# A decode-attention kernel whose tensor-engine work becomes one loop of seven rounds

## The chip, the core and the metric

One core of a Trainium2 chip runs the whole kernel. The metric is the time of one execution on the device in microseconds (us), the median of several. The span in a profile is about 2 us shorter than that time (252.3 against 254.14 us in the profiled run of the kernel before). A core has five engines, each with its own instruction stream: PE (matrix multiply), DVE (vector), ACT (scalar functions), POOL (general), SP (here it only issues transfers). Sixteen transfer (DMA) engines move data between the device memory (HBM) and the core's SBUF. PE writes to PSUM; the kernel uses eight banks of 128 x 2 KB there.

## The reference

Two independent attention layers, A and B, each decoding one token. Both have 32 query heads, 16 key/value heads of 128 columns, a cache of 8192 positions, a 576-wide input. A looks only at the last 2048 positions, B at all of them.

```python
q = x @ wq                                  # 576 -> 32 heads x 128
k, v = cache (A: the last 2048 rows; B: all 8192), each head shared by 2 query heads
p = softmax(q @ k.T * 128 ** -0.5)
out = (p @ v).reshape(1, 4096) @ wo         # 4096 -> 576
result = concatenate([A, B])
```

All tensors are bf16. About 102.8 MB have to be read: 20 blocks of K and 20 of V of 2 MB each (4 of each for A, 16 for B), and four weight matrices of 4.7 MB.

## The kernel before

A small scheduler (`Program`) holds a list of operations with the resources they read and write, and derives the semaphore waits. Each engine has one semaphore that only counts up, so a wait is "at least n", once per dependency:

```python
def run(name, eng):
    seen = {}
    for op in per[name]:
        want = {}
        for o in op.deps:
            key = ("d", o.dma_sem) if o.dma_sem is not None else ("e", o.eng)
            want[key] = max(want.get(key, 0), o.value)
        for key in sorted(want):
            if seen.get(key, 0) >= want[key]:
                continue
            ...
            eng.wait_ge(sem, want[key])
        ins = op.fn(eng)
        ...
```

All loads go through a ring of 6 SBUF slots of 2 MB. For K, PE turns each block round (64 transposes of 128 x 128 through four PSUM banks, which ACT and DVE copy out to `kt`) and multiplies it with the queries. For V, PE multiplies with the transposed probabilities. Everything is written out in order, nothing is looped:

```python
def k_phase(P, c, between):
    pend = None
    for i in range(NS[P]):
        s = load_kv(ks, P, c, i)
        for half in range(2):
            u = k_transpose(s, half)          # 32 transposes, 4 copies
            if pend is not None:
                k_scores(P, *pend)
            pend = (i, half, u)
        between(i)                            # V blocks of the chunk before
    k_scores(P, *pend)
    return softmax_exp(P, c)

q_phase(0)
pa = k_phase(0, 0, lambda i: None)            # A: 4 K blocks
q_phase(1)
pb0 = k_phase(1, 0, between_b0)               # B, first 4096 rows; 3 of A's V blocks between
...                                           # cut: B's second chunk, output weights of A,
                                              # the last 8 V blocks, output weights of B
```

Of the kernel before, what the change touches and what calls it, by code (L numbers as in the profile page):

```python
# [6 lines left out]
U32 = mybir.dt.uint32  # L7
# [12 lines left out]
NSLOT = 6  # L20
NKT = 3
TS = 64
WQ_UNITS = 9
WQ_SLOT = 4
OUTW = DM // 4


class Op:
    def __init__(self, eng, fn, reads, writes, dma_sem=None):
        self.eng, self.fn, self.reads, self.writes = eng, fn, reads, writes  # L30
        self.dma_sem = dma_sem
        self.deps = []
        self.needed = False
        self.value = None


class Program:

# [4 lines left out]
    def __init__(self, nc):  # L43
        self.nc = nc
        self.ops = []
        self.writer = {}
        self.readers = {}
        self.sems = {e: nc.alloc_semaphore("done_" + e) for e in self.ENGINES}
        self.dma_sems = {}
        self.dma_count = {}  # L50

    def add(self, eng, fn, reads=(), writes=(), dma=None, after=()):
        op = Op(eng, fn, tuple(reads), tuple(writes), dma)
# [19 lines left out]
        for o, raw in deps:  # L73
            if o is op:
                continue
            if o.dma_sem is None and o.eng == eng and (not raw or eng in ("pe", "sp")):
                continue
            op.deps.append(o)
            o.needed = True
        if dma is not None:  # L80
            if dma not in self.dma_sems:
                self.dma_sems[dma] = self.nc.alloc_semaphore("dma_" + dma)
                self.dma_count[dma] = 0
            self.dma_count[dma] += 16
            op.value = self.dma_count[dma]
        self.ops.append(op)
        return op

    def emit(self):
        count = {e: 0 for e in self.ENGINES}  # L90
        for op in self.ops:
            if op.dma_sem is None and op.needed:
                count[op.eng] += 1
                op.value = count[op.eng]
        per = {e: [o for o in self.ops if o.eng == e] for e in self.ENGINES}

        def run(name, eng):
            seen = {}
            for op in per[name]:
                want = {}  # L100
                for o in op.deps:
                    key = ("d", o.dma_sem) if o.dma_sem is not None else ("e", o.eng)
                    want[key] = max(want.get(key, 0), o.value)
                for key in sorted(want):
                    if seen.get(key, 0) >= want[key]:
                        continue
                    seen[key] = want[key]
                    sem = self.dma_sems[key[1]] if key[0] == "d" else self.sems[key[1]]
                    eng.wait_ge(sem, want[key])
                ins = op.fn(eng)  # L110
                if op.dma_sem is not None:
                    ins.then_inc(self.dma_sems[op.dma_sem], 16)
                elif op.needed:
                    ins.then_inc(self.sems[op.eng], 1)
# [23 lines left out]
def bass_concat_heads__sliding_block_cached__gqa_block_cached__decode_kernel(  # L138
# [19 lines left out]
    S_len = [W_A, SK]  # L158
    base = [SK - W_A, 0]
# [3 lines left out]
    PH = [128 // G[P] for P in range(2)]  # L163
    CH = [TS * PH[P] for P in range(2)]
    NCH = [S_len[P] // CH[P] for P in range(2)]
    UW = [8 * PH[P] for P in range(2)]
    CW = [2 * UW[P] for P in range(2)]
    NS = [HKV // G[P] for P in range(2)]
# [4 lines left out]
    slots = nc.alloc_sbuf_tensor("slots", [128, NSLOT, SLOT], BF16)  # L173
    kt = nc.alloc_sbuf_tensor("kt", [128, NKT, UNIT], BF16)
    ptm = nc.alloc_sbuf_tensor("ptm", [128, 2, 32 * 512], BF16)
# [7 lines left out]
    qtm = nc.alloc_sbuf_tensor("qtm", [128, 2, HKV * 32], BF16)  # L183
    xtwo = nc.alloc_sbuf_tensor("xtwo", [128, 2, 8], BF16)
    xpad = nc.alloc_sbuf_tensor("xpad", [128, 2, 10, 32], BF16)
    par = [None, None, nc.alloc_sbuf_tensor("par2", [128, 2], F32), None, nc.alloc_sbuf_tensor("par4", [128, 4], F32)]
# [3 lines left out]
    acc = nc.alloc_sbuf_tensor("acc", [128, 3, DH], F32)  # L190
# [9 lines left out]
    misc_bf = misc[:, :].bitcast(BF16)  # L200
# [17 lines left out]
    def setup(pool):  # L218
        def zero(t):
            return pool.memset(t, 0.0)  # L220
        zero(ident[:])
        zero(xpad[:])
        zero(selq[:])
        pool.memset(onesf[:], 1.0)
        zero(warm[:])
        return zero(qtm[:])

    add("pool", setup, writes=["ident", ("xpad", 0), ("xpad", 1), "selq", "ones", "warm", ("qtm", 0), ("qtm", 1)])
# [7 lines left out]
    for b in range(2):  # L236
        for h in range(8):
            add("pool", lambda pool, b=b, h=h: pool.memset(ptm[:, b, h * 2048:(h + 1) * 2048].bitcast(U32), 0),  # L238
                writes=[("ptm", b)])

    def setup2(pool):
        pool.memset(identf[:], 0.0)
        pool.memset(pick[:], 0.0)
        pool.memset(same[:], 0.0)
        return pool.memset(opj[:], 0.0)

    add("pool", setup2, writes=["identf", "pick", "same", ("opj", 0), ("opj", 1)])
# [3 lines left out]
    for dj in range(-3, 4):  # L251
        add("pool", select(same[:], 32 * dj, [[-1, 128]], 1), reads=["same"], writes=["same"])

    for n in (2, 4):
        add("dve", lambda dve, n=n: dve.tensor_reduce(par[n][:, :], ident[:, :].rearrange("p (m g) -> p g m", g=n),
                                                      AX.X, ALU.add),
            reads=["ident"], writes=[("par", n)])

    add("act", lambda act: act.activation(warm[:, 4:8], warm[:, 0:4], ACT.Exp), reads=["warm"], writes=["warm2"])


    slot_n = [0]

    def load(src_of, view_of, what):
        s = slot_n[0] % NSLOT
        slot_n[0] += 1
        res = ("slot", s)
        add("sp", lambda sp: sp.dma_start(view_of(slots[:, s, :]), src_of()), writes=[res], dma="slot%d" % s)
        return s

    def load_wq(P, k):
        lo, hi = k * WQ_SLOT * 2048, min(WQ_UNITS, (k + 1) * WQ_SLOT) * 2048
        return load(lambda: wqs[P].rearrange("(m r) n -> m (r n)", m=64)
                    .rearrange("m (e y) -> (m e) y", e=2)[:, lo:hi],
                    lambda v: v[:, 0:hi - lo], "wq")

    def load_kv(arrs, P, c, i):
        r0 = base[P] + c * CH[P]

        def src():  # L280
            a = arrs[P]
            return a[0, i * G[P]:(i + 1) * G[P], r0:r0 + CH[P], :].rearrange("g (p t) d -> p g (t d)", t=TS)
        return load(src, lambda v: v, "kv")


    def load_wo(P, lo, parts):
        s = slot_n[0] % NSLOT
        slot_n[0] += 1
        o, made = 0, []
        for k, rows in enumerate(parts):  # L290
            n = rows * DM
            res = ("slot", s) if len(parts) == 1 else ("slot", s, k)

            def go(sp, lo=lo, n=n, o=o):
                return sp.dma_start(slots[:, s, o:o + n],
                                    wos[P].rearrange("(p j) n -> p (j n)", p=128)[:, lo * DM:lo * DM + n])
            add("sp", go, writes=[res], after=[("slot", s)], dma="slot%d" % s if res == ("slot", s) else "part%d_%d" % (s, k))
            made.append((lo, lo + rows, s, o, res))
            lo += rows
            o += n  # L300
        return made


    def x_columns(P):
        for e in range(2):
            add("dve", lambda dve, e=e: dve.tensor_scalar(xpad[:, P, 5 * e:5 * e + 5, 0], xtwo[:, P, 0:5],  # L306
                                                          par[2][:, e:e + 1], None, ALU.mult),
                reads=[("xtwo", P), ("par", 2)], writes=[("xpad", P)])
# [4 lines left out]
    def q_part(P, k, s):  # L313
        def mm(pe):
            for u in range(k * WQ_SLOT, min(WQ_UNITS, (k + 1) * WQ_SLOT)):
                for c in range(2):
                    for j in range(4):
                        n = 2 * j + c
                        x = u // 2 if n // 4 == u % 2 else 5 + (u + 1) // 2
                        o = (u - k * WQ_SLOT) * 2048 + (n % 4) * 512  # L320
                        ins = pe.matmul(qps[c][32 * j:32 * j + 32, :], lhsT=xpad[:, P, x, :],  # L321
                                        rhs=slots[:, s, o:o + 512], start=(u == 0), stop=(u == WQ_UNITS - 1))
            return ins
        add("pe", mm, reads=[("xpad", P), ("slot", s)], writes=qbank)

    def q_finish(P):
# [11 lines left out]

        def put(dve):
            row = 2 * HKV * 32  # L340
            for e in range(2):
                dst = bass.AP(tensor=qtm, offset=P * HKV * 32 + e, ap=[[row, 128], [34, 4], [136, 4]])
                src = opsum[:, 0:32].rearrange("p (a e j) -> p a e j", a=4, e=2)[:, :, e, :]
                ins = dve.tensor_copy(dst, src)
            return ins
        add("dve", put, reads=[B_O], writes=[("qtm", P)])


    k_count = [0]

    def k_transpose(s, half):
# [181 lines left out]
    def k_phase(P, c, between):  # L533
        pend = None
        for i in range(NS[P]):
            s = load_kv(ks, P, c, i)
            for half in range(2):
                u = k_transpose(s, half)
                if pend is not None:
                    k_scores(P, *pend)  # L540
# [92 lines left out]
```

## Time and profile before

| | before |
|---|---|
| time, median of 3 (lowest to highest) | 254.39 us (254.33 to 254.62) |
| span of the profiled run | 252.3 us |
| read from HBM | 102.76 MB |
| busy share: PE, DVE, ACT | 66%, 32%, 35% |
| instruction fetches of PE's queue | 27 packets, 0.44 MB |
| last output weights: first engine done, last engine done | 242.9 us, 249.2 us |
| span's end after the last landing | 3.1 us |

Lines of the profile's page. Each digit is the busy share of one of 40 slices of the span (6.3 us each), in tenths; PEclk is the granted PE clock in tenths; GB/s is what the DMA engines moved in each slice. The last two lines are DMA queues with packets, MB and their share of the sixteen engines' span.

```profile
PEclk9999999999979999599998897789997755555557
DMA  7999999999999999999999999999999999999971
GB/s 273 400 450 418 431 431 407 433 431 423 420 434 423 421 434 418 423 434 420 423 431 426 418 431 429 423 418 439 423 422 423 428 423 429 426 426 425 415 309 56
...
q1 hardware_dynamic: 7936, 102.77, 96.4%
q8 instruction: 27, 0.44, 0.7%
```

The transfers run without a gap at about 425 GB/s. The reader should look at the last two numbers, 309 and 56: the transfers fade out instead of stopping.

The same place in windows of 1 us, the last three columns being the granted clock, the busy share of the DMA engines, and GB/s:

```profile
242.00:243.00 1.00, 0.84 (x4) 0.70 (x4) 0.12 (x1) 0.00 (x0) 0.00 (x0) 0.50 0.91 351
243.00:244.00 1.00, 0.79 (x28) 0.82 (x32) 0.07 (x1) 0.00 (x0) 0.00 (x0) 0.50 0.53 213
...
247.00:248.00 1.00, 0.43 (x16) 0.25 (x16) 0.00 (x0) 0.00 (x0) 0.00 (x0) 1.00 0.33 113
248.00:249.00 1.00, 0.51 (x20) 0.31 (x20) 0.00 (x0) 0.00 (x0) 0.00 (x0) 1.00 0.09 35
```

From 243 us half of the engines have nothing left, and the other half works on. Each transfer raises its semaphore once per engine, so the trace says when each of the sixteen was done with it. For three transfers, the delay of each engine behind the first (worked out from those semaphore events):

```
lands at  28.7 us: 0 .11 .12 .18 .20 .20 .23 .25 .27 .28 .28 .29 .35 .41 .42 .43
lands at 137.6 us: 0 .23 .24 .25 .30 .31 .86 1.4 1.8 1.9 3.2 3.2 3.2 3.2 3.3 3.5
lands at 242.9 us: 0 .23 .27 .30 .35 .85 .90 1.4 4.7 4.7 4.8 4.8 5.0 5.1 6.2 6.2
```

The kernel ends with the slowest engine. Eight engines are late at the end, six by 4.7 to 5.1 us and two by 6.2 us; three fetches each for the six and four for the two would make the 26 fetches made by then, at about 1.6 us each (an estimate from these lags; the trace doesn't tell which engine moved a fetch). Last, lines of the chain of waits (start, duration, what) in A's K blocks: 32 transposes and the scores, twice per block.

```profile
25.15 3.59 PE ktps L358 x64
28.75 1.03 PE sacc L381 x12
29.77 1.89 PE ktps L358 x32
31.67 1.01 PE sacc L381 x15
```

### The profile page before, as it was taken

Reading aid. Unit: us, or ns where it says so; the run is one execution under the profiler, and the core shown is the slowest. Engines: PE = TensorE matmul, PEld = TensorE weight load, DVE = VectorE, ACT = ScalarE, POOL = GpSimd, SP = SyncE. Lnnn points to the kernel's source line nnn. Section 1 sums busy time; section 2 is a strip of 40 time slices with the busy share of each in tenths; the row PEclk is TensorE's granted clock in tenths of the full one; section 3 lists DMA queues with packets and bytes.
Section 4 is the critical chain, followed back from the end, with each engine's and each line's share of the span. In section 5 each row is a group of like instructions: output and inputs, shape, how many; then the busy total and the mean of one; then the engine's idle time right before and its main releaser. Section 6 shows DMA issues by size and latency. Waiting matters only on the chain.

```text
span 252.3 us, 7334 instructions
## 1 busy us (share of the span) xinstructions
PE 165.5 (66%) x3438; PEld 129.3 (51%) x3438; DVE 81.0 (32%) x141; ACT 87.2 (35%) x92; POOL 22.9 (9%) x45
## 2 busy tenths in 40 slices
PE   0008999787799995888893784956934535333573
PEld 0004877466588873766673563735723534222551
DVE  0391544327544552256541340422434000000010
ACT  2000766545466673365662361533630000000000
POOL 8996000000000000000000000000000000000000
PEclk9999999999979999599998897789997755555557
DMA  7999999999999999999999999999999999999971
GB/s 273 400 450 418 431 431 407 433 431 423 420 434 423 421 434 418 423 434 420 423 431 426 418 431 429 423 418 439 423 422 423 428 423 429 426 426 425 415 309 56
DMA packets 8254, 103.24 MB, mean 409 GB/s; under 512 B 1184, under 2 KB 1312, under 8 KB 2080
## 3 DMA queue, kind: packets, MB, share of 16 engines
q1 hardware_dynamic: 7936, 102.77, 96.4%
q8 instruction: 27, 0.44, 0.7%
q10 hardware_dynamic: 288, 0.00, 0.1%
q14 instruction: 3, 0.02, 0.0%
HBM read 102.76 MB, written 0.00 MB: 407 GB/s over the span
## 4 chain that ended last, share of the span: by engine, by line
DMA 61%; PE 29%; DVE 6%; issue 1%; ACT 0%; SPq 0%
DMA slots<-in_B_k_cache_dram 21%; DMA slots<-in_B_v_cache_dram 19%; PE ktps L358 15%; DMA slots<-in_B_wo_dram 10%; DMA slots<-in_A_v_cache_dram 8%; PE sacc L381 5%; DMA xtwo<-in_A_x_dram 4%; DVE xpad L306 3%; PE opsum L483 2%; PE opsum L321 2%; PE misc L321 2%; PE misc L517 2%; DVE ptm L426 1%; PE misc L415 1%; PE misc L463 1%
## 5 line engine op out<-in xcount | busy, mean ns | idle before, releaser
L364 ACT ACTIVATE kt<-ktps 128x1024 bf16<-128x1024 bf16 x80 | 77.8, 1022 | 65.6 <-PE ktps L358 65.5
L358 PE MATMUL ktps<-ident,slots 128*128 128x128 bf16 x1280 | 85.3, 230 | 19.6 <-DMA slots<-in_B_k_cache_dram 19.6
L358 PEld LDWEIGHTS ktps<-ident,slots 128*128 128x128 bf16 x1280 | 78.8, 104 | 32.7 <-DMA slots<-in_B_k_cache_dram 20.8
L367 DVE COPY kt<-ktps 128x1024 bf16<-128x1024 bf16 x80 | 55.3, 691 | 79.4 <-PE ktps L358 79.2
L483 PE MATMUL opsum<-slots,ptm 128*32 128x128 bf16 x1280 | 28.3, 256 | 29.8 <-DMA slots<-in_B_v_cache_dram 29.2
L483 PEld LDWEIGHTS opsum<-slots,ptm 128*32 128x32 bf16 x1280 | 24.6, 115 | 36.1 <-DMA slots<-in_B_v_cache_dram 33.1
L381 PE MATMUL sacc<-kt,qtm 128*32 128x512 bf16 (+1 forms) x384 | 30.8, 418 | 0.3 <-DVE kt L367 0.3
L321 PE MATMUL opsum<-slots,xpad 128*32 128x512 bf16 x72 | 8.1, 427 | 19.9 <-DVE xpad L306 19.9
L238 POOL MEMSET ptm<- 128x1024 uint32 x16 | 14.3, 951 | 0.0
L321 PEld LDWEIGHTS opsum<-slots,xpad 128*32 128x32 bf16 x72 | 2.3, 105 | 22.4 <-issue 21.3
L497 DVE TENSOR_SCALAR acc<-opsum,stat 128x128 f32<-128x128 f32 x2 | 0.7, 346 | 40.5 <-PE opsum L483 40.5
L381 PEld LDWEIGHTS sacc<-kt,qtm 128*32 128x32 bf16 x384 | 7.0, 99 | 7.0 <-ACT kt L364 1.1
L306 DVE TENSOR_SCALAR xpad<-xtwo,par 128x5 bf16<-128x5 bf16 x4 | 8.1, 3941 | 7.1 <-DMA xtwo<-in_A_x_dram 7.1
L517 PE MATMUL misc<-slots,opj 128*32 128x144 bf16 x256 | 8.1, 303 | 2.6 <-DMA slots<-in_B_wo_dram 1.9
L327 ACT ACTIVATE qrow<-opsum 128x512 bf16<-128x512 f32 x2 | 1.2, 597 | 23.0 <-PE misc L321 23.0
L517 PEld LDWEIGHTS misc<-slots,opj 128*32 128x32 bf16 x256 | 6.7, 135 | 3.9 <-DMA slots<-in_B_wo_dram 3.5
L404 ACT ACTIVATE psb<-sacc,stat 128x2048 bf16<-128x2048 f32 x3 | 5.9, 1967 | 7.8 <-DVE stat L398 7.8
L576 POOL MEMSET ptm<- 128x512 uint32 x1 | 0.5, 525 | 86.3 <-PE opsum L483 86.3
L321 PE MATMUL misc<-slots,xpad 128*32 128x512 bf16 x72 | 8.0, 421 | 0.0
L426 DVE TENSOR_SCALAR ptm<-misc,par 128x256 bf16<-128x256 bf16 (+1 forms) x16 | 6.9, 527 | 3.3 <-PE misc L415 3.3
L415 PE MATMUL misc<-ident,psb 128*128 128x128 bf16 x48 | 3.8, 221 | 3.7 <-DVE ptm L426 3.7
L415 PEld LDWEIGHTS misc<-ident,psb 128*128 128x128 bf16 x48 | 2.7, 98 | 5.3 <-DVE ptm L426 4.2
(50 smaller groups left out, 37.0 us busy)
## 6 DMA issues: line engine op xcount, KB each, us to landing
slots<-in_B_k_cache_dram SPq DMA_DIRECT2D x16, 2048.0 KB, 22.2
slots<-in_B_v_cache_dram SPq DMA_DIRECT2D x16, 2048.0 KB, 25.0
slots<-in_A_k_cache_dram SPq DMA_DIRECT2D x4, 2048.0 KB, 19.3
slots<-in_A_v_cache_dram SPq DMA_DIRECT2D x4, 2048.0 KB, 20.8
slots<-in_A_wq_dram SPq DMA_DIRECT2D x2, 2048.0 KB, 9.7
slots<-in_B_wq_dram SPq DMA_DIRECT2D x2, 2048.0 KB, 19.0
slots<-in_A_wo_dram SPq DMA_DIRECT2D x2, 2016.0 KB, 25.4
slots<-in_B_wo_dram SPq DMA_DIRECT2D x1, 2016.0 KB, 28.4
```

What stands on the lines that cost most here:

```text
L238: add("pool", lambda pool, b=b, h=h: pool.memset(ptm[:, b, h * 2048:(h + 1) * 2048].bitcast(U32), 0), writes=[("ptm", b)])
L306: add("dve", lambda dve, e=e: dve.tensor_scalar(xpad[:, P, 5 * e:5 * e + 5, 0], xtwo[:, P, 0:5], par[2][:, e:e + 1], None, ALU.mult), read ...
L321: ins = pe.matmul(qps[c][32 * j:32 * j + 32, :], lhsT=xpad[:, P, x, :], rhs=slots[:, s, o:o + 512], start=(u == 0), stop=(u == WQ_UNITS - 1))
L358: ins = pe.matmul(ktps_bf[q][:, t * 128:(t + 1) * 128], lhsT=slots[:, s, o:o + 128], rhs=ident[:, :], start=True, stop=True, is_transpose= ...
L364: add("act", lambda act, q=q, dst=dst: act.activation(dst, ktps_bf[q], ACT.Copy), reads=[("bank", q)], writes=[("kt", u, q)])
L367: add("dve", lambda dve, q=q, dst=dst: dve.tensor_copy(dst, ktps_bf[q]), reads=[("bank", q)], writes=[("kt", u, q)])
L381: ins = pe.matmul(sacc[32 * j:32 * j + 32, o:o + w], lhsT=qtm[:, P, g * 32:(g + 1) * 32], rhs=rhs, start=(g == 0 and o % 512 == 0), stop=( ...
L404: return act.activation(psb[:, 0:w * G[P]].rearrange("p (x g) -> p x g", g=G[P]), src, ACT.Exp, bias=st(P, C_NB + c), scale=SCALE, accum_o ...
L415: ins = pe.matmul(misc_bf[:, t * 128:(t + 1) * 128], lhsT=psb[:, o:o + 128], rhs=ident[:, :], start=True, stop=True, is_transpose=True)
L426: ins = dve.tensor_scalar(dst, src, par[G[P]][:, e:e + 1], None, ALU.mult)
L483: ins = pe.matmul(opsum[32 * j:32 * j + 32, 0:DH], lhsT=ptm[:, pb, o:o + 32], rhs=slots[:, s, b * 128:(b + 1) * 128], start=(i == 0 and u ...
L517: ins = pe.matmul(misc[32 * j:32 * j + 32, 0:OUTW], lhsT=opj[:, P, jj:jj + 32], rhs=slots[:, s, o:o + OUTW], start=(jj == 0), stop=(jj == ...
```

## The change

The intent: PE's program gets short. K and V get four slots each at fixed addresses, A is treated as one more chunk of B's shape with a mask, and PE's K and V work becomes one loop of seven rounds: round g does K of group g (g < 5) and V of group g - 2 (g >= 2), with branches round what a round does not do. As the body is the same in every round, the waits can't compare with ever growing counts: each wait takes its count off the semaphore again. The core of the diff (cut; the helper that works out the counts, the mask, the zeroing of the score banks and the extraction of V's diagonal are left out):

```diff
-NSLOT = 6
-NKT = 3
+NS = 4
+NKT = 4
...
+        def looped(eng, ops):
+            waits, before = self.waits_of_loop(ops)
...
+            with eng.Fori(0, rounds) as i:
+                def some(todo):
+                    for place in todo:
+                        for key, (n, take) in sorted(waits.get(place, {}).items(), ...):
+                            ins = eng.wait_ge(self.sem(key), n)
+                            if take:
+                                ins.then_inc(self.sem(key), -n)
+                        one(eng, body[place])
+                while places:
+                    cond = body[places[0]].loop[2]
...
+                        with eng.If(cond(i)):
+                            some(places[:n])
...
-    slots = nc.alloc_sbuf_tensor("slots", [128, NSLOT, SLOT], BF16)
+    kslots = nc.alloc_sbuf_tensor("kslots", [128, NS, SLOT], BF16)
+    vslots = nc.alloc_sbuf_tensor("vslots", [128, NS, SLOT], BF16)
...
+    for P in range(2):
         x_columns(P)
...                                        # both query products come first now
+    ORDER = ["k0", "k1", "k2", "v0", "v1", "k3", "v2", "v3"]
+    for g in range(5 + LAG):
+        for what in ORDER:
+            s = int(what[1])
+            if what[0] == "k" and g < 5:
+                load_kv(ks, g, s, kslots, "k", ...)
+            if what[0] == "v" and g >= LAG:
+                load_kv(vs, g - LAG, s, vslots, "v")
...
+            for u in range(2, 6):
+                k_scores(g, u - 2, 2 * u)
+                k_transpose(g, u, 2 * u + 1)
...
+    weights(0)
     weights(1)
+    for P in range(2):
+        combine(P)
...                                        # both output products at the end
```

## The prediction

> **What bounds the kernel now.** Transfers. The page's rows by slice show DMA at 9 tenths nearly throughout, about 425 GB/s, while PE is busy 66%, DVE 32%, ACT 35%. 102.8 MB at 425 GB/s is 242 us of a 252.3 us span. The rest is the start (2 us), the end (3.1 us after the last landing) and a tail: in windows of 1 us the DMA share is 1.0 until 243, about 0.5 until 247, 0.09 at 248. Completions of the last weight transfer by engine: the first at 242.9, eight within 1.4 us of it, six 4.7 to 5.1 us and two 6.2 us late. At 29 us all were within 0.4 us; the lag grows in steps.
>
> **Its cause.** The table of DMA queues lists instruction fetches: 27 packets, 16 KB each, about 1.07 us. They come once per 256 PE instructions, from 29.6 us to the end. The lags summed over the eight late engines, 39 us, over the 26 fetches until the tail, give 1.5 us per fetch (an estimate). Fetching PE's 6876 matmuls and weight loads costs the slowest engine four fetches, 6 us, and the kernel ends with the slowest engine.
>
> **The change.** Bytes, transfer sizes, transposes, score and V matmuls stay. Added: 24 zeroing matmuls, a mask pass and about 1.4 us per V group on DVE; removed: 14.3 us of POOL memsets. None is on the transfers' path. What matters is PE's static program: about 340 instructions ahead, 1250 in the loop, 580 after: 9 blocks of 256 instead of 27. [...]
>
> - Loop stays resident (65%): about 8 fetches, one per late engine, perhaps two: lag 1.5 to 3 us instead of 6.2. Gain 3 to 4.7 us.
> - Each round refetches (35%): 40 to 50 fetches, lag 7.5 to 10 us, and a stall at each back edge: 257 to 262 us.
>
> **A bubble.** Rounds 0 and 1 load K only, into 4 slots. A K slot costs PE 5.8 us (twice 1.89 us transposes and 1.02 us scores, chain of waits) against 4.9 us of transfer. So the third K of round 2 is issued near 72 us, with 2 us of transfers left in the queue; then V loads refill it. I expect 0 to 2 us of idle DMA near 65 to 80 us. Later 8 slots are ahead and PE needs 29 us of 39.
>
> **Sum.** Fastest engine 242.9, spread 0.4, lag 1.5 to 3, bubble 0.5, end 3.1: span about 249; the time is 2.1 us above the span: 251.3 us. Range 248.9 to 259.5, skewed for refetching. Without any fetch 248.5 is about the floor, so over 2% faster (below 249.3) has 9%; within 2%, 76%; slower, 15%.
>
> **What would show it.** Instruction queue: 8 to 10 packets (right) or over 40 (wrong). Spread of the last transfer's completions at most 3 us; DMA share near 1.0 until about 244. DMA share below 0.9 between 65 and 80 us if the bubble is there. PE idle at each round's start if branches fetch.
>
> **What would make it wrong.** Refetching; branch stalls in the K-only rounds, which have little slack; slow waits in the loop; a throttled clock there.

No trace then had a loop or a branch in it, so the 65% for a resident loop, and the 35% for refetching with its stalls, are estimates. 242.9 + 0.4 + 1.5 to 3 + 0.5 + 3.1 is 248.4 to 249.9, about 249, and with the 2.1 us above the span it came to 251.3 us.

## The result, and the profile after

| | before | after |
|---|---|---|
| time, median of 4 (lowest to highest) | 254.50 us (254.33 to 254.69) | 260.57 us (260.01 to 261.28) |
| span of the profiled run | 252.3 us | 259.5 us |
| instruction fetches of PE's queue | 27 | 8 |
| last output weights: first engine done | 242.9 us | 254.3 us |
| spread to the last engine | 6.2 us | 1.7 us |
| span's end after the last landing | 3.1 us | 3.5 us |

The change is slower by a ratio of 1.024 (95% interval 1.021 to 1.027). A ratio here is the mean time of one kernel's fast runs over that of the other's of the same rounds, so it isn't quite the ratio of the quoted medians.

The three rows of landings add up to the difference of the spans: +11.4 us for the first engine, -4.6 us of spread, +0.4 us at the end, together +7.2 us. So the spread shrank as expected, and 11.4 us were lost somewhere before. (Two cautions: the engines that ran dry lost their lag, the spread being 2.12 us for the transfer that began to land at 59.3 us and 0.33 us for the one at 78.8 us, so the 1.7 us is judged better from e2 below, which has no hole and 2.1 us. And the profiled run is the slowest of the four: the other spans are 258.2 to 258.8 us, so the loss is about 1 us less in a usual run.) The same lines of the page as shown of before:

```profile
PEclk9996589957799999995998586899599555555577
DMA  7999999995478999999999999999999999999992
GB/s 280 394 450 414 434 429 414 442 419 182 200 283 330 422 427 428 437 424 429 432 422 437 424 427 432 422 437 427 424 434 419 437 427 424 434 420 433 429 400 87
...
q1 hardware_dynamic: 7936, 102.77, 94.3%
q8 instruction: 8, 0.13, 0.2%
```

Queue q8 has 8 packets instead of 27, and the fade-out is gone (400, then the end). But four slices, from 58 to 84 us, moved 182 to 330 GB/s. The end in windows of 1 us, last columns as before:

```profile
253.00:254.00 1.00, 0.62 (x21) 0.53 (x24) 0.19 (x1) 0.00 (x0) 0.00 (x0) 0.50 1.00 388
254.00:255.00 1.00, 1.00 (x44) 1.00 (x36) 0.00 (x0) 0.00 (x0) 0.00 (x0) 0.50 0.44 154
255.00:256.00 1.00, 1.00 (x45) 1.00 (x37) 0.00 (x0) 0.00 (x0) 0.00 (x0) 0.50 0.04 14
```

The engines now stop together, within 2 us. The hole, in windows of 5 us (PE, PEld, DVE, ACT, POOL busy with counts, then clock, DMA share, GB/s):

```profile
50.00:55.00 5.00, 2.79 (x31) 2.56 (x31) 0.69 (x1) 2.05 (x2) 0.00 (x0) 0.65 1.01 426
55.00:60.00 5.00, 3.90 (x35) 2.95 (x36) 1.38 (x2) 1.02 (x1) 0.24 (x1) 0.50 0.80 341
60.00:65.00 5.00, 3.46 (x45) 2.00 (x43) 3.18 (x4) 1.02 (x1) 0.24 (x1) 0.82 0.64 210
65.00:70.00 5.00, 2.61 (x36) 2.46 (x34) 1.51 (x4) 4.84 (x5) 0.00 (x0) 0.86 0.55 229
70.00:75.00 5.00, 5.00 (x71) 4.24 (x70) 3.17 (x7) 1.76 (x3) 0.00 (x0) 0.80 0.45 141
75.00:80.00 5.00, 5.00 (x86) 3.91 (x84) 2.85 (x5) 3.96 (x5) 0.24 (x1) 1.00 0.87 333
```

PE issued 31 to 45 matmuls in a window where it issues 85 when it isn't held up, and the DMA engines run dry a few us later: a load of K needs a slot that PE has finished reading (SP's loads waited 15 times for PE's transposes, 88.0 us in all). PE's own timeline in that stretch (start, duration, line, what, count, and in brackets the idle time before it and its releaser; L449 are transposes, L469 scores, L208 is the line that emits the loop's waits):

```profile
45.87 1.96 PE L449 MATMUL ktps<-ident,kslots 128*128 128x128 bf16 x32
47.76 0.63 PE L469 MATMUL sacc<-kt,qst 128*32 128x512 bf16 x8
50.78 2.79 PE L449 MATMUL ktps<-ident,kslots 128*128 128x128 bf16 x31 [2.39 <-PEq L208]
56.10 0.29 PE L449 MATMUL ktps<-ident,kslots 128*128 128x128 bf16 x1 [2.52 <-issue]
56.32 1.04 PE L469 MATMUL sacc<-kt,qst 128*32 128x512 bf16 x8
57.29 3.59 PE L449 MATMUL ktps<-ident,kslots 128*128 128x128 bf16 x32
60.82 1.58 PE L469 MATMUL sacc<-kt,qst 128*32 128x512 bf16 x16
63.93 1.95 PE L449 MATMUL ktps<-ident,kslots 128*128 128x128 bf16 x32 [1.54 <-PEq L208]
68.28 3.29 PE L449 MATMUL ktps<-ident,kslots 128*128 128x128 bf16 x32 [2.39 <-PEq L208]
```

Four holes of 1.5 to 2.5 us stand in rounds 0 and 1. The trace's control instructions and fetches go with three of them. At 47.1 us PE executes the branch round the V part: it took 3.20 us, and a 16 KB instruction fetch ran from 47.9 to 48.9 us inside it. In the middle of a group of transposes PE's stream stops at 53.3 us; a fetch runs at 53.7 us. The branch at 61.8 us took 1.27 us, with a fetch at 60.7 us. In later rounds the same branches, when taken, took 0.20 to 0.21 us, and the loop's jump back took 0.23 us at 63.2 us already. Branches that were not taken took 0.07 to 0.08 us, and the four that PE took forward in round 0 took 0.37, 3.20, 0.32 and 1.27 us. After the fetch at 66.7 us there is none until 250.5 us, though the loop ran to 234.6 us and a round had up to 1257 recorded PE instructions: the body was not fetched again; the first pass over it is what costs. The fourth hole, at 65.9 us, is another matter: the copy that frees the transposes' bank waits on ACT behind the exponential, as the timelines of DVE (mask, maximum) and then of ACT (exponential, then the copies) show:

```profile
62.44 1.23 DVE L497 TENSOR_TENSOR sacc<-sacc,maskS 128x1024 f32<-128x1024 f32 x1 [0.83 <-PE sacc L469]
63.71 1.22 DVE L498 TENSOR_REDUCE stat<-sacc 128x1 f32<-128x1024 f32 x1
```

```profile
65.16 1.97 ACT L506 ACTIVATE psb<-sacc,stat 128x2048 bf16<-128x2048 f32 x1 [4.06 <-DVE stat L500]
...
67.12 2.95 ACT L455 ACTIVATE kt<-ktps 128x1024 bf16<-128x1024 bf16 x3
```

The holes were not the whole cost. The group of 32 transposes at 57.3 us took 3.59 us, not 1.96: the granted clock is 0.50 in that window. It fell at 51.6 us, after the hole of 2.4 us that ended at 50.8 us, and was back at 1.0 at 61.8 us; what made it fall is not shown. The seven K loads from 37 us on show the sum of it. This line of SP's timeline spans them; the last, the third K load of round 2, which the prediction puts near 72 us, was issued at 83.0 us:

```profile
37.15 46.42 SPq L368 DMA_DIRECT2D kslots<-in_B_k_cache_dram  x7
```

### The profile page after: what moved, and what is told of

The parts are those of the page before. It is cut to its first block, busy times and chain, and to the rows that moved or that the text cites. A ratio compares the mean times of both kernels' runs of the same rounds, so it can differ in the third digit from the quotient of the medians.

```text
span 259.5 us, 7521 instructions
## 1 busy us (share of the span) xinstructions
PE 172.1 (66%) x3406; PEld 134.3 (52%) x3406; DVE 80.9 (31%) x152; ACT 87.5 (34%) x92; POOL 12.9 (5%) x49
## 5 line engine op out<-in xcount | busy, mean ns | idle before, releaser
L449 PE MATMUL ktps<-ident,kslots 128*128 128x128 bf16 x1280 | 89.8, 236 | 23.6 <-PEq L208 21.0
L449 PEld LDWEIGHTS ktps<-ident,kslots 128*128 128x128 bf16 x1280 | 83.2, 107 | 39.7 <-issue 39.7
L540 PE MATMUL opsum<-vslots,ptm 128*32 128x128 bf16 x1280 | 28.4, 257 | 32.8 <-PEq L208 32.8
L540 PEld LDWEIGHTS opsum<-vslots,ptm 128*32 128x32 bf16 x1280 | 24.9, 116 | 38.5 <-issue 37.0
L469 PE MATMUL sacc<-kt,qst 128*32 128x512 bf16 x320 | 27.0, 411 | 0.9 <-issue 0.5
L403 PE MATMUL opsum<-vslots,xpad 128*32 128x512 bf16 x64 | 8.4, 508 | 16.8 <-DVE xpad L388 11.3
L469 PEld LDWEIGHTS sacc<-kt,qst 128*32 128x32 bf16 x320 | 5.3, 95 | 6.9 <-issue 3.0
L403 PE MATMUL misc<-vslots,xpad 128*32 128x512 bf16 x64 | 8.5, 512 | 0.0
L626 PE MATMUL ktps<-kslots,opj 128*32 128x144 bf16 x184 | 5.3, 305 | 0.8 <-DVE opj L614 0.8
L626 PEld LDWEIGHTS ktps<-kslots,opj 128*32 128x32 bf16 x184 | 4.9, 137 | 1.0 <-issue 1.0
```

The lines of the kernel that those rows point to most:

```text
L403: ins = pe.matmul(qps[c][32 * j:32 * j + 32, :], lhsT=xpad[:, P, x, :], rhs=src[:, o:o + 512], start=(u == 0), stop=(u == WQ_UNITS - 1))
L449: ins = pe.matmul(ktps_bf[q][:, t * 128:(t + 1) * 128], lhsT=kslots[:, s, o:o + 128], rhs=ident[:, :], start=True, stop=True, is_transpose ...
L469: ins = pe.matmul(sacc[32 * j:32 * j + 32, 512 * half:512 * half + 512], lhsT=qst[:, s * 64 + e * 32:s * 64 + e * 32 + 32], rhs=rhs, start ...
L540: ins = pe.matmul(opsum[32 * j:32 * j + 32, s * DH:(s + 1) * DH], lhsT=ptm[:, o:o + 32], rhs=vslots[:, s, b * 128:(b + 1) * 128], start=(u ...
L626: ins = pe.matmul(ktps[P][32 * j:32 * j + 32, 0:OUTW], lhsT=opj[:, P, jj:jj + 32], rhs=view[:, o:o + OUTW], start=(jj == 0), stop=(jj == H ...
```

## The experiments

The theory at this point (theory 1): the hole in the transfers comes from PE's stalls on its first pass through the loop, in the two K-only rounds, where only four K slots buffer; and the fewer fetches are worth the 4.6 us of spread. Each experiment is the change with the edit shown. e1 to e4 ran together on one chip, then e5 to e7 and then e8 on another; the kernel before took 254.56 us with the first, 254.45 and 254.51 us with the others. Results of all are in one table at the end of this section. "Gap" is how much later than in the kernel before (242.94 us) the first engine was done with the last output weights.

### e1_unroll: the rounds written out

```diff
...                                               # cut: static() emits an operation and its waits
+            for r in range(PEEL):                 # PEEL = 7: all rounds
+                for place in places:
+                    cond = body[place].loop[2]
+                    if cond is None or cond(r):
+                        static(place)             # same waits, same counts taken off
+            if PEEL == rounds:
+                return
-            with eng.Fori(0, rounds) as i:
+            with eng.Fori(PEEL, rounds) as i:
```

> PE's 7 rounds are written out (same instructions, waits and takes, no branch, no loop); load order as in the change. Theory 1 (the gap in the transfers comes from PE stalling at branches on the first pass over the loop's code, with only 4 K slots ahead): no stall near 47, 53 and 62 us, the gap of the engines shrinks from 11 us to 2 to 4 us (late start of K and the wait for the exponential stay), but 26 to 28 fetches are back and the completions of the last transfer spread over 6 us: 256 to 258 us. Rival A (the loop's waits that take counts off are slow): they are all still there, gap of 8 us or more and the lag on top: 263 us or more. Rival B (two K-only rounds on 4 slots starve the transfers whatever the branches do): as rival A, 263 us.

Measured: 261.74 us (257.95 to 262.04, one run slow), ratio 1.021, interval 1.012 to 1.029. 27 fetches, spread 5.3 us, gap 7.7 us. Theory 1 missed by 4 us, though one run of the four, at 257.95 us, lies in its range. The gap shrank by 3.7 us only, though no branch was left; rival A's 8 us came nearer than theory 1's 2 to 4. The trace has new holes where a 256-instruction block begins. From 52.0 us PE starts no instruction for 3.26 us, and the fetch of that block starts only at 52.6 us. PE's executed count there is 961; other stops come at 2241, 2497 and 4801, all 63 short of a multiple of 256. So PE waited for its own straight-line code. The profile of the kernel before has no such stop. The one at 52.0 us, in the middle of a group of 32 transposes:

```profile
50.88 1.29 PE L465 MATMUL ktps<-ident,kslots 128*128 128x128 bf16 x20
55.22 1.46 PE L465 MATMUL ktps<-ident,kslots 128*128 128x128 bf16 x12 [3.05 <-issue]
```

### e2_early_v: four V loads one round earlier

```diff
-            if what[0] == "v" and g >= LAG:
-                load_kv(vs, g - LAG, s, vslots, "v")
+            if what[0] == "v" and (g == 1 or g > LAG):
+                load_kv(vs, max(g - LAG, 0), s, vslots, "v")
```

> The loop as in the change, but the four V loads of group 0 are issued in round 1 between its K loads and not in round 2. Theory 1: the stalls on the first pass stay (about 7 us of PE), but the transfers have 4 more free slots while PE is late, so no slice between 55 and 85 us under 0.95 DMA share; 8 fetches, last spread under 3 us: 249.5 to 251 us, faster than before by 1.5 to 2%. Rival A: PE is slow in every round, so the gap moves to rounds 2 to 4: 255 us or more.

Measured: 251.51 us (251.34 to 252.29), ratio 0.989, interval 0.987 to 0.991; 8 fetches, spread 2.1 us, gap 0.1 us. The page's lines show no hole:

```profile
GB/s 260 416 440 423 428 425 420 438 417 428 425 420 434 425 428 428 427 433 425 428 425 430 433 425 428 425 430 433 428 423 433 430 428 428 423 432 423 429 383 30
...
q8 instruction: 8, 0.13, 0.2%
```

PE's first-pass holes are still there (2.0, 3.7 and 5.0 us between 48 and 67 us, the last with the wait for the exponential in it), and PE is as late as in the change: the third K load of round 2 was issued at 82.7 us. They cost nothing, because four V loads stand in the queue meanwhile. That settles how the stalls became time: through the load order, which leaves the four V slots empty in rounds 0 and 1. The median is 0.5 us above the expected range; the span ended 4.6 us after the last landing and not 3.1. e5 takes that up.

### e3_early_v_unroll: both

The edits of e1 and e2 together.

> Both: V loads early and the rounds written out. Theory 1: no gap, but 26 to 28 fetches and a spread of about 6 us at the last transfer: 254 to 255.5 us, as the kernel before, 4 to 5 us slower than e2. Rival C (the fetches are not what makes the engines drift apart; the order of loads and the number of slots are): spread as in e2, 250 to 251 us.

Measured: 257.88 us (255.89 to 262.11, one slow run), ratio 1.011. 27 fetches, but a spread of 2.2 us and a gap of 5.5 us. Neither theory 1 nor rival C: PE stood still at eight block boundaries, some 27 us in all (worked out from the trace), the transfers ran dry near 185 us, and engines that ran dry lost their lag in the change (a spread of 2.12 us became 0.33 us), so the spread says nothing here. The question from e1 is sharper now: what makes a fetch come late when the code is straight?

### e4_peel2: only rounds 0 and 1 written out

`PEEL = 2` in the edit of e1.

> Rounds 0 and 1 written out, rounds 2 to 6 looped; load order as in the change. Theory 1: no stall in the K-only rounds, gap 2 to 4 us; 13 or 14 fetches, two on the slowest engine, spread 3 to 4 us: 253 to 255 us, between e1 and e2. Rivals A and B: gap 8 us or more, 259 to 262 us.

Measured: 258.52 us (256.31 to 260.79, one slow run), ratio 1.009. 14 fetches, spread 3.0 us, gap 7.0 us. The fetches and the spread came as expected, the gap (2 to 4 us expected) and the time did not: as in e1, PE stopped at 52 us for 3.26 us at a block boundary. Writing out the K-only rounds doesn't cure them.

### The second theory

For each fetch one can measure the time from PE's first executed instruction of a block to the start of the next block's fetch. Its median is 2.9 us in the kernel before and 4.5 us in e1 and e3 (highest tenth: 3.7 us against 7 us and more), and a block of 256 instructions lasts about 8 us of K work or 4 us of V work when PE is busy (worked out from 2.46 us for 80 and 1.9 us for 128 instructions). What differs is the waits. In the kernel before, 197 of PE's waits ride on a weight load, that is, are part of it, and 29 are instructions of their own. In e1 27 ride and 231 stand alone, 223 of them taking counts off. Theory 2: with waits of their own, PE asks for the next block later, and often too late. That is the guess which e6 to e8 put to the test; why it should be so is not shown, as the traces have the fetches and not the asking. Rival D: fetches are slow because more transfers are queued.

### e5_tail: the end reordered (with e2)

```diff
-    weights(0)
-    weights(1)
+    together(lambda: weights(0), lambda: weights(1))    # step by step side by side, B in its own bank
+    together(lambda: combine(0), lambda: combine(1))
     for P in range(2):
-        combine(P)
```

> e2 with the end reordered: the softmax weights of A and B step by step side by side (B's in another PSUM bank), then both combines, then both output products. In e2 the last weight landed at 245.1 us and the span ended at 249.7, 4.6 us later, with the chain that ended last running from the last V landing through weights, combine, output product, combine, output product. Theory: that serial chain, not the transfers, ends e2; overlapping it takes 4 to 5 us off it, so the span ends about 3.1 us after the last landing again as in the kernel before: 249.5 to 250.5 us. Rival: the end is set by the landing of the last output weights and their matmuls at the slow clock: 251 to 251.5 us as e2.

Measured: 249.76 us (249.68 to 250.03), ratio 0.981, interval 0.980 to 0.983. Lines of the chain that ended last, first of e2, where it is PE and DVE work from the last V block to the end, then of e5, where it is a transfer again:

```profile
236.61 3.76 PE ktps L626 x128
...
240.40 0.31 DVE outsb L632
...
243.57 3.70 PE ktps L626 x119
```

```profile
216.42 28.92 DMA vslots<-in_B_wo_dram
...
245.38 0.28 PE ktps L642 x4
```

The span ends 2.8 us after the last landing. This is the fastest version, 1.7 to 2.0% faster than the kernel before by the interval.

### e6_early_v_plain: cumulative waits, V early, rounds written out

```diff
-            looped(eng, ops[lo:hi])
+            plain(eng, ops[lo:hi])        # wait_ge(sem, total so far), nothing taken off
...                                        # cut: and the edit of e2
```

> As e3 (V early, rounds written out), but the waits are the cumulative ones of the kernel before: no counts are taken off, so a wait can ride on the instruction that follows. In e3 PE stood still for 3 to 5 us where a 256-instruction block began before its fetch had come (executed counts 2497, 4801). Theory 2: waits that take counts are instructions of their own[...], so each fetch is asked for too late; without them the stalls go and the time is that of the kernel before, 254 to 255.5 us, with 26 to 28 fetches and a last spread of 5 to 6 us. Rival D: fetches come late because 8 slots of transfers are queued and not 5; then the stalls stay: 257 to 259 us.

Measured: 255.01 us (254.68 to 255.79), ratio 1.002. 26 fetches, spread 6.4 us, first engine done at 242.91 us: no gap. The scatter of e3 is gone, too.

```profile
GB/s 277 394 433 420 436 419 432 427 417 440 418 425 432 425 432 422 421 425 427 425 425 432 414 425 432 422 430 422 419 438 419 427 430 419 429 425 424 421 280 31
...
q8 instruction: 26, 0.43, 0.7%
```

This line against that of e2 is the cleanest pair: same loads, same order, first engine done within 0.1 us of each other, but 26 fetches against 8, a fade-out at the end (280, 31), and the last engine 4.2 us later. That is what the fetches cost, and what the loop saves: PE's waits differ too, but both runs move the same data. Theory 2 holds against rival D: eight slots of transfers are queued here as well. A few late fetches are left (three, 8.7 us in all), in rounds with enough loads ahead.

### e7_plain: cumulative waits, load order of the change

The edit of e6 without that of e2.

> As e1 (load order of the change, rounds written out) with the cumulative waits. Theory 2: no stall at block boundaries in the K-only rounds; what remains of the gap in the transfers is K starting 2 to 3 us late and PE's wait for the exponential in round 1 (2 to 4 us), gap 3 to 5 us against 11 in the change; 256.5 to 258.5 us. Rival D, and rival B (K-only rounds on 4 slots starve the transfers anyway): as e1, 260 to 262 us.

Measured: 257.51 us (256.90 to 258.12), ratio 1.011. 26 fetches, gap 2.7 us; no stop at a block boundary in the K-only rounds, one hole of 3.9 us in the wait for the exponential. The third K load of round 2 was issued at 73.9 us. So the two K-only rounds on four slots cost 2.7 us by themselves, somewhat more than the 0 to 2 us of the prediction. Rival B, that they starve whatever the branches do, is refuted as the main cause.

### e8_waits_alone: e6 with each wait of PE's seven rounds an instruction of its own

The edit against e6, as it is in effect:

```diff
-                    eng.wait_ge(self.sem(key), op.left[key][1])
+                    eng.wait_ge(self.sem(key), op.left[key][1]).then_inc(self.sem(("pe", "scratch")), 1)
```

> e6 with one difference: every wait of PE's seven rounds also adds 1 to a semaphore nobody reads, so it has to stay an instruction of its own (246 of them) and can't ride on the next weight load as 216 of the 246 do in e6. Nothing is taken off. Theory 2a ([...]fetches are asked for late): as e3, stalls at block boundaries, first engine done with the last weight after 245 us, 256 to 259 us with a wide scatter. Theory 2b (it is the taking off that is slow): as e6, 254.5 to 255.8 us.

Measured: 257.24 us (256.37 to 258.75), ratio 1.012. PE has 222 waits of its own and 24 that ride (e6: 30 and 216). The first engine was done at 248.5 us (gap 5.5 us, as in e3), the median delay of a fetch is 4.5 us (e6: 2.9), and PE stands at eight block boundaries for 31 us in all. The transfers run dry again:

```profile
GB/s 273 396 431 426 430 433 422 422 430 427 428 429 420 422 435 426 422 422 420 427 430 422 427 422 425 430 430 422 422 407 335 399 376 394 425 427 426 428 398 37
```

Nothing is taken off in e8, so the taking off isn't needed for the slowness: it comes as well with 222 waits of their own that add to a semaphore.

| run | edit | time, us | ratio | fetches | first engine | gap | spread |
|---|---|---|---|---|---|---|---|
| before | | 254.4 to 254.6 | 1 | 27 | 242.9 | 0 | 6.2 |
| after | loop | 260.57 | 1.024 | 8 | 254.3 | 11.4 | 1.7 |
| e1_unroll | written out | 261.74 | 1.021 | 27 | 250.7 | 7.7 | 5.3 |
| e4_peel2 | two rounds written out | 258.52 | 1.009 | 14 | 249.9 | 7.0 | 3.0 |
| e7_plain | written out, riding waits | 257.51 | 1.011 | 26 | 245.7 | 2.7 | 7.3 |
| e2_early_v | loop, V early | 251.51 | 0.989 | 8 | 243.0 | 0.1 | 2.1 |
| e3_early_v_unroll | written out, V early | 257.88 | 1.011 | 27 | 248.5 | 5.5 | 2.2 |
| e6_early_v_plain | riding waits, V early | 255.01 | 1.002 | 26 | 242.9 | 0.0 | 6.4 |
| e8_waits_alone | e6, waits alone | 257.24 | 1.012 | 27 | 248.5 | 5.5 | 1.8 |
| e5_tail | e2, end reordered | 249.76 | 0.981 | 8 | 243.0 | 0.0 | 2.4 |

Times are medians with all runs. The columns from "fetches" on are of the one profiled run of each.

## Why the prediction was right or wrong

**The bound and the lag: right.** Transfers bound the kernel, and the spread at its end is made by PE's instruction fetches. e2 and e6 differ in fetches (and in how PE waits) and not in loads, and the last engine lands 4.2 us apart.

**The loop stays resident: right.** About 8 fetches were predicted, 8 came; spread of at most 3 us predicted, 1.7 measured; a gain of 3 to 4.7 us, 4.6 measured. The hole flatters these two; e2, without a hole, gives a spread of 2.1 us and a last engine done 4.1 us earlier than before, and bears the forecast out. There was no refetching, the prediction's main worry (no fetch between 66.7 and 250.5 us); that it would stay away was an estimate.

**The bubble: wrong, and it is the step that failed.** The prediction had "0 to 2 us of idle DMA near 65 to 80 us", with the third K load of round 2 issued "near 72 us". It was issued at 83.0 us, and the bubble, 0.5 us in the sum, cost 11.4 us. The mechanism was named (K-only rounds, four slots, PE behind), and "branch stalls in the K-only rounds, which have little slack" was listed among what would make the prediction wrong, as were "slow waits in the loop" and "a throttled clock there", but the sum held nothing for them: for the looped case it counted fetches, not the wait for each on the first pass. In the series e7, e1, after (2.7, 7.7, 11.4 us of gap) the 11.4 us split as follows. All are differences of single profiled runs, of which e7's and the change's were the slowest of their four, and e1 scatters by 4 us from run to run, so the sizes are rough:

- 2.7 us belong to the K-only rounds as such: late start of K and the wait behind mask, maximum and exponential. The prediction had 0 to 2 us.
- About 5.0 us (e1 less e7) come from waits that are instructions of their own, so that straight code arrives late.
- About 3.7 us (after less e1) come from the loop's branches on the first pass. That such stalls happen is seen directly (3.20 and 1.27 us for branches that later take 0.2).

The 5.8 us for a K block were also off: they were read from A's blocks of the kernel before, where 16 matmuls of 256 columns score half a block in 1.02 us. B's form, which the loop uses for A too, scores it in 0.56 us; a block takes 4.9 us when nothing stalls, no more than its transfer. That error went the other way. So it is partly luck that e7's third K load of round 2, at 73.9 us, came near the 72 us: over seven blocks, 0.9 us too much each stood in for a wait for the exponential (3.9 us) and a stretch at half clock that the sum left out.

**The range: wrong on its upper side.** Slower by over 2% had 15%, but mainly for refetching, which did not happen.

**The rest.** That the epilogue fits behind the output weights was only just true: the end after the last landing grew from 3.1 to 3.5 us, and in e2 to 4.6 us, until e5 reordered it.

What stays open: how PE asks for its next block isn't in the trace. That own waits delay the asking for a block is inferred from e6 against e8 and from the delays of the fetches. e8 also issues some 190 instructions more than e6 (51 ns each in the change's trace) and adds to a semaphore; no run has the waits of PE's rounds standing alone without changing a semaphore, so what exactly delays the asking stays open.

## What to carry to other kernels

When transfers are the bound, count instruction fetches as transfers and look at the completion of the last load engine by engine: code that is fetched once and then looped can be worth several us (8 fetches in e2 against 26 in e6, and 4.2 us between their last engines). But the first pass over this loop had stalls, and jumping over parts of it was slow (up to 3.20 us for a branch that later takes 0.2): let the first rounds have loads queued ahead, not the thinnest buffering of the whole run. And semaphore waits that stand alone were not free here (222 of them in e8 against 30 in e6, and 2.2 us); the 223 waits of the change that take counts off all stood alone.
